# Fixed-order attention: q, k, v ahead of weights, conversions at other places, variance in PSUM, first outputs behind the last results

## The chip, the core and the metric

The kernel runs on one core of a Trainium2 chip. The metric is the device time of one execution in microseconds; the kernel before has a median of 1237.65 us over 3 runs (1236.31 to 1238.02). The engines named below are TensorE (PE, its weight loads PEld), VectorE (DVE), ScalarE (ACT), GpSimd (POOL) and SyncE (SP), whose queue issues the DMAs.

## What is computed

Three stages follow one another. All inputs and the output are float32.

```
# q, k, v: (batch 4, heads 8, seq 576, dim 64)
kv  = einsum('bhsd,bhse->bhde', k, v)
out = einsum('bhsd,bhde->bhse', q, kv)
x   = out / sqrt(mean(out*out, -1) + 1e-6) * g_norm
x   = x.transpose(0, 2, 1, 3).reshape(2304, 512)
# first feed-forward: 512 -> 2048 -> 512
h   = x @ w_in
x   = (h * clip(h + 3, 0, 6) / 6) @ w_out
# four weighted experts: 512 -> 1024 -> 512
p   = domain_probs / (domain_probs.sum(-1) + 1e-9)
y   = sum over e of p[:, e] * (relu(x @ w1[e]) @ w2[e])
```

## The kernel before, in words

The kernel works with pairs: a value is held as a high part in a rounded float32 form that PE takes at full rate, and a low part, the difference. A product of two such values is three matmuls (high-high, high-low, low-high). ACT usually writes the high part (a copy), DVE the low part (a subtraction).

**Attention.** The 4 batches times 2 halves of heads give eight steps, i = 0 to 7. att_load(i) issues three DMAs of 576 KB (q, k, v) into six rotating SBUF tiles, so the loads of step i+2 wait until step i has read its own. att_q transposes q on PE into PSUM and hands back ACT copies; att_kv forms k^T v in the PSUM tile kvp (72 small matmuls) and copies it to kvd; att_out (L233) multiplies q by kv into the PSUM tile pp, of which there is one, then ACT squares it and DVE reduces the squares. att_rms forms 1/rms in small steps (L271 to L279, 18 columns each) and scales pp into the SBUF tile xt. att_x (L283) transposes xt back on PE into PSUM tiles px (two of 512 columns, one of 128, px8), and ACT and DVE write from them the pair xH, xL that the feed-forward reads.

**Feed-forward.** w_in and w_out are cut into 16 column tiles, numbered n; each has two halves (h = 0 for w_in, h = 1 for w_out). load_raw issues the DMA of one half (512 KB, three SBUF buffers); convert(n) turns it into a pair by seven DVE operations and three ACT copies per half, written as a generator whose yields let the caller place it step by step. Where POOLED covers (n, h), the multiply and the add of that half (L161, L164) run on POOL. conv(k) takes k such yields. Tokens are cut into tiles t = 0 to 4 (512 columns, the last 256). ff_in(u, t, f) is twelve matmuls into a PSUM tile ph and a gate of four operations (L336 to L340, ACT and DVE in turn) that gives gH, gL; ff_out is twelve matmuls into four PSUM banks po, and ff_end copies them to acc for the first unit (L372) and adds them to acc for later units.

**Order.** From L462 to L539 the order of PE, ACT and DVE instructions is written out by hand (manual_schedule). Each step i of the loop from L472 takes att_out(i), the transposes of q(i+1), the small steps of 1/rms, att_kv(i+1), then filler for PE (zero matmuls, warm, in steps 0 and 1; from step 2 the first unit's ff_in, half of its matmuls in an even step and half with the gate in the odd one), then the transposes of the last result, att_x(i-1), and SLOTS[i] yields of conversion. After the eight steps att_x(7) follows; then the attention's PSUM pools close and a pool of six banks (psb) opens over their space; then ff_out(0, t) for t = 0 to 4 with the two remaining ff_in between them and conv(3) after each (L519), and small operations on domain_probs. From L541 on step(n) runs the other four units: an ff_in, an ff_out three items behind, and as much conversion as a budget allows; that part, and the experts after it, are ordered by the planner, which may move some of its instructions up into the end of the hand-written part.

Of the kernel before, what the change touches and what calls it, by code (L numbers as in the profile page):

```python
# [8 lines left out]
F32 = mybir.dt.float32  # L9
# [8 lines left out]
def kernel(  # L18
# [18 lines left out]
    nc = tc.nc  # L37
# [27 lines left out]
    PADL, PADR = 208, 248  # L65
# [25 lines left out]
    def bank_b(shape, name):  # L91
        turn[0] += 1
        return psb.tile(shape, F32, tag=f"b{turn[0] % 6}", name=name)
# [40 lines left out]
    def convert(n):  # L134
# [4 lines left out]
        for h in range(2):  # L139
# [29 lines left out]
            load_raw()  # L169
# [88 lines left out]
    def att_rms(i):  # L258
# [3 lines left out]
        va, s0, r0, ri = (sp.tile([P, NG], F32, tag=n, name=n) for n in ("va", "s0", "r0", "ri"))  # L262
# [20 lines left out]
    def att_x(i, pxs, px8):  # L283

        b, hf = divmod(i, 2)
        xt = st.pop(i)["xt"]
# [8 lines left out]
        for r in range(NP):  # L295
# [5 lines left out]
            em.append(pair(px, xH[b][:, hf * NP + r, :], xL[b][:, hf * NP + r, :]))  # L301
        nc.tensor.transpose(px8, xt[:, 2 * GA:].rearrange("p g d -> p (g d)"), ident)
# [44 lines left out]
    def ff_out(u, t, f):  # L347
# [4 lines left out]
        if f == 0:  # L352
            po_t[u, t] = [bank_b([P, TB], "po2")[:, :n] for _ in range(KD)]
# [11 lines left out]
    def ff_end(u, t):  # L365
# [42 lines left out]
    POOLED = ((0, 1), (3, 0))  # L408
# [31 lines left out]
    def warm(sizes):  # L440
        zp = psa.tile([P, DM], F32, tag="a0", name="zp")
        for n in sizes:
            nc.tensor.matmul(zp[:, :n], lhsT=zero[:, :P], rhs=zero[:, :n], start=True, stop=True)
# [404 lines left out]
```

## Time and profile before

| | |
|---|---|
| median of 3 runs | 1237.65 us |
| profiled execution | 1240.38 us, of which its span 1238.60 us |
| mean granted clock of PE | 0.937 of full speed |
| PE busy | 1209.9 us, 98% of the span |
| DVE busy | 769.6 us, 62% |
| ACT busy | 583.4 us, 47% |
| POOL busy | 14.0 us, 1% |
| moved by DMA | 87.15 MB, mean 70 GB/s |

The profile comes from one execution. Times count from the span's start. A row of the timeline gives the start, the length, the engine, the line, the operation and the tile written and read; in brackets stands how long the engine was idle before and what released it. [...]

### The profile page before, as it was taken

The page shows a single profiled execution, that of the slowest core. Times are in us where ns is not written, and L with a number is a line of the kernel's source. Part 1 is how long each engine was busy: PE and PEld are TensorE (multiplying, and loading weights), DVE is VectorE, ACT ScalarE, POOL GpSimd, SP SyncE. Part 2 cuts the span into 40 slices and gives each one's busy share as a digit, 9 for nine tenths or more (in the row PEclk, how much of TensorE's full clock was granted, in tenths as well). Part 3 has the DMA queues.
Part 4 walks back from the last instruction along what each step waited for, and adds up shares of the span by engine and source line. Part 5 has one row for each costly group of instructions (what it writes and reads, how often), then busy time and mean ns, then how long its engine had stood idle before and what let it go on. Part 6 is the DMA issues. An engine that isn't in the chain of part 4 may idle for free.

```text
span 1238.6 us, 16911 instructions
## 1 busy us (share of the span) xinstructions
PE 1209.9 (98%) x6749; PEld 1067.7 (86%) x6749; DVE 769.6 (62%) x1448; ACT 583.4 (47%) x1121; POOL 14.0 (1%) x20
## 2 busy tenths in 40 slices
PE   8978999999999999999999999999999999999997
PEld 7766888888888889999999989999999899999996
DVE  5865999783533555565656585656565856565652
ACT  5756455442322434444444554444444554444441
POOL 1100000000000000000000000000000000000000
PEclk9868999999999999999999999999999999999998
DMA  9611222210010002111212232112222321222202
GB/s 357 226 35 35 85 71 86 66 52 1 1 68 1 1 1 69 69 69 69 69 68 69 69 103 85 69 68 69 69 68 68 86 103 68 69 69 68 69 1 51
DMA packets 59343, 87.15 MB, mean 70 GB/s; under 512 B 3712, under 2 KB 36480, under 8 KB 59264
## 3 DMA queue, kind: packets, MB, share of 16 engines
q1 hardware_dynamic: 59264, 86.07, 21.0%
q8 instruction: 53, 0.87, 0.3%
q14 instruction: 26, 0.21, 0.0%
HBM read 81.34 MB, written 4.72 MB: 69 GB/s over the span
## 4 chain that ended last, share of the span: by engine, by line
PE 93%; DVE 3%; DMA 2%; ACT 1%; issue 0%; SPq 0%; POOLq 0%; POOL 0%; ACTq 0%; DVEq 0%
PE po L682 31%; PE po L358 15%; PE qa L715 14%; PE qb L715 14%; PE ph L323 5%; PE ph L324 5%; PE ph L325 5%; DMA vin<-in_v_dram 1%; DMA kin<-in_k_dram 1%; PE pp L242 1%; DVE acc L698 1%; PE kvp L224 1%; DVE xl L292 1%; PE pq L205 0%; PE px L299 0%; ACT acc L372 0%
## 5 line engine op out<-in xcount | busy, mean ns | idle before, releaser
L682 PE MATMUL po<-wout,g 128*128 128x512 f32 x1728 | 402.1, 390 | 0.0
L682 PEld LDWEIGHTS po<-wout,g 128*128 128x128 f32 x1728 | 323.6, 188 | 65.4
L715 PE MATMUL qb<-xs,win 128*128 128x384 f32 x1008 | 203.3, 336 | 1.2 <-ACT us L756 1.2
L715 PE MATMUL qa<-xs,win 128*128 128x384 f32 x1008 | 203.0, 335 | 0.0
L358 PE MATMUL po<-gH,w 128*128 128x512 f32 (+1 forms) x640 | 195.9, 372 | 4.6 <-DVE xl L292 3.0
L715 PEld LDWEIGHTS qb<-xs,win 128*128 128x128 f32 x1008 | 177.9, 188 | 3.8 <-ACT us L756 1.8
L715 PEld LDWEIGHTS qa<-xs,win 128*128 128x128 f32 x1008 | 178.2, 188 | 2.2 <-ACT us L756 0.2
L589 DVE TENSOR_TENSOR wout<-raw,wout 128x512 fp32r<-128x512 f32 x96 | 62.2, 688 | 171.0 <-ACT wout L588 171.0
L588 ACT ACTIVATE wout<-raw 128x512 fp32r<-128x512 f32 x96 | 55.4, 625 | 226.5 <-PE po L682 226.5
L358 PEld LDWEIGHTS po<-gH,w 128*128 128x128 f32 x640 | 118.3, 190 | 26.3 <-issue 3.3
L323 PE MATMUL ph<-xh,w 128*128 128x512 f32 (+1 forms) x320 | 119.6, 374 | 2.4 <-DVE r L337 2.4
L358 PE MATMUL po<-gL,w 128*128 128x512 f32 (+1 forms) x320 | 118.8, 371 | 0.0
L324 PE MATMUL ph<-xl,w 128*128 128x512 f32 (+1 forms) x320 | 118.4, 370 | 0.0
L325 PE MATMUL ph<-xh,w 128*128 128x512 f32 (+1 forms) x320 | 118.3, 370 | 0.0
L336 ACT ACTIVATE r<-ph,three 128x512 f32<-128x512 f32 (+1 forms) x80 | 51.6, 645 | 140.1 <-PE ph L325 140.0
L337 DVE SCALAR_TENSOR_TENSOR r<-r,ph 128x512 f32<-128x512 f32 (+1 forms) x80 | 50.5, 632 | 101.5 <-ACT r L336 101.2
L745 DVE SCALAR_TENSOR_TENSOR g<-sums,g 128x384 fp32r<-128x384 f32 x96 | 53.5, 558 | 81.4 <-ACT g L742 81.4
L742 ACT ACTIVATE g<-cs 128x384 fp32r<-128x384 f32 x96 | 50.4, 525 | 63.7 <-DVE cs L758 54.4
L588 ACT ACTIVATE win<-sums 128x512 fp32r<-128x512 f32 x96 | 60.7, 632 | 40.2 <-DVE sums L601 37.7
L323 PEld LDWEIGHTS ph<-xh,w 128*128 128x128 f32 x320 | 61.0, 190 | 13.6 <-DVE r L337 2.9
L745 DVE SCALAR_TENSOR_TENSOR g<-cs,g 128x384 fp32r<-128x384 f32 x96 | 53.3, 555 | 27.2 <-ACT g L742 27.2
L324 PEld LDWEIGHTS ph<-xl,w 128*128 128x128 f32 x320 | 61.0, 191 | 10.1
(106 smaller groups left out, 1260.6 us busy)
## 6 DMA issues: line engine op xcount, KB each, us to landing
raw<-in_moe_w_dram SPq DMA_DIRECT2D x96, 512.0 KB, 4.2
raw<-in_moe_w_in_dram SPq DMA_DIRECT2D x16, 512.0 KB, 3.6
raw<-in_moe_w_out_dram SPq DMA_DIRECT2D x16, 512.0 KB, 3.6
qin<-in_q_dram SPq DMA_DIRECT2D x8, 576.0 KB, 6.8
kin<-in_k_dram SPq DMA_DIRECT2D x8, 576.0 KB, 7.0
vin<-in_v_dram SPq DMA_DIRECT2D x8, 576.0 KB, 8.2
out_dram<-acc SPq DMA_DIRECT2D x36, 128.0 KB, 2.4
dp<-in_moe_domain_probs_dram SPq DMA_DIRECT2D x2, 36.0 KB, 8.5
```

Of the source, the lines that this page charges most:

```text
L323: nc.tensor.matmul(ph, lhsT=w[:, 0, c, :], rhs=xH[t][:, c, :], start=(c == 0), stop=False)
L324: nc.tensor.matmul(ph, lhsT=w[:, 0, c, :], rhs=xL[t][:, c, :], start=False, stop=False)
L325: nc.tensor.matmul(ph, lhsT=w[:, 1, c, :], rhs=xH[t][:, c, :], start=False, stop=(c == KD - 1))
L336: lambda: nc.scalar.activation(out=r, in_=ph, func=AF.Relu, bias=three[:, 0:1]),
L337: lambda: nc.vector.scalar_tensor_tensor(out=r, in0=r, scalar=6.0, in1=ph, op0=ALU.min, op1=ALU.mult),
L358: nc.tensor.matmul(po_t[u, t][o], lhsT=lhsT, rhs=rhs, start=(f == 0 and m == 0), stop=(f == UF[u] - 1 and m == 2))
L588: nc.scalar.activation(out=dst[0], in_=src, func=AF.Copy)
L589: nc.vector.tensor_tensor(out=dst[1], in0=src, in1=dst[0].bitcast(F32), op=ALU.subtract)
L682: nc.tensor.matmul(ps[i], lhsT=lhsT, rhs=w[:, f, y], start=(j == 0 and f == 0 and m == 0), stop=(j == FP - 1 and f == 1 and m == 2))
L715: nc.tensor.matmul(bank, lhsT=w[:, wy, AOP[m], c], rhs=xs[m][:, xy, c], start=first and n == 0, stop=n == 5, skip_group_check=True)
L742: nc.scalar.activation(out=g[f][:, 0, t], in_=src, func=func)
L745: nc.vector.scalar_tensor_tensor(out=g[f][:, 1, t], in0=src, scalar=0.0, in1=g[f][:, 0, t].bitcast(F32), op0=ALU.max, op1=ALU.subtract)
```

## The change

The first load of weights is issued behind q, k, v of step 0, and one load less is issued before the loop; two loads are added inside it, at steps 1 and 3. The nine yields of conversion ahead of att_q(0) go, three behind att_kv(0) become six, the yields per step change, and four instead of three follow each item of the transition. Other halves go to POOL: (0,0), (0,1), (1,0). The variance va becomes 18 columns of the PSUM tile pp. Step 1 transposes result 0 ahead of its zero matmuls, and step 7 transposes result 6 ahead of its filler and leaves that result's px8 and most of its own gate for later. Half of the first tile's outputs are formed in kvp while step 7 is being scaled, the other half in psx and psa; the last transposes go into pp. From tile 1 on DVE copies the fourth output of the first unit.

```diff
-    PADL, PADR = 208, 248
+    PADL, PADR = 232, 248
-        return psb.tile(shape, F32, tag=f"b{turn[0] % 6}", name=name)
+        return psb.tile(shape, F32, tag=f"b{(turn[0] - 1) % 6}", name=name)
...
-            load_raw()
+            if (n, h) > (0, 0):
+                load_raw()
...
-        va, s0, r0, ri = (sp.tile([P, NG], F32, tag=n, name=n) for n in ("va", "s0", "r0", "ri"))
+        s0, r0, ri = (sp.tile([P, NG], F32, tag=n, name=n) for n in ("s0", "r0", "ri"))
+        va = pp[:, 3 * TB - NG:]
...
-        for r in range(NP):
+        for r in range(len(pxs)):
...
+        if px8 is None:
+            return em
+        st.pop(i)
...
-        if f == 0:
-            po_t[u, t] = [bank_b([P, TB], "po2")[:, :n] for _ in range(KD)]
+        if f == 0 and (u, t) not in po_t:
+            po = [bank_b([P, TB], "po2")[:, :n] for _ in range(KD)]
+            po_t[u, t] = [po[o] for o in (0, 2, 3, 1)] if (u, t) == (0, 1) else po
...
-            if u == 0:
+            if u == 0 and o < KD - 1:
                 nc.scalar.activation(out=acc[t][:, o, :], in_=p, func=AF.Copy)
+            elif u == 0:
+                nc.vector.tensor_copy(out=acc[t][:, o, :], in_=p)
...
-    POOLED = ((0, 1), (3, 0))
+    POOLED = ((0, 0), (1, 1))
...
-    warm([DM] * 8)
-
-    load_raw()
+    warm((0,) * 8)
+
     att_load(0)
...
-    SLOTS = {0: 3, 1: 3, 2: 4, 3: 4, 4: 4, 5: 4, 6: 4, 7: 4}
+    SLOTS = {0: 8, 1: 2, 2: 3, 3: 0, 4: 3, 5: 1, 6: 3, 7: 0}
...
-        conv(9)
         qc = att_q(0)
...
-        warm([DM] * 6)
+        warm((0,) * 4)
         att_kv(0)
         qc[2]()
-        warm([DM] * 2)
-        conv(3)
+        warm((0,) * 2)
+        conv(6)
...
+            if i in (1, 3):
+                load_raw()
...
+            kvp = st[min(i + 1, NHB - 1)]["kvp"]
+            em = []
+            if i and not (2 <= i < NHB - 1):
+                pxs = ...
+                em = att_x(i - 1, pxs, kvp[:, 1, 2 * P:3 * P] if nxt else None)
             if i < 2:
-                warm(((480,) * 3 + (504,) * 3 + (506,) * 2, (248,) * 3 + (250,) * 3 + (288,) * 3 + (368,) * 3)[i])
+                warm(((8,) * 3 + (64,) * 3, (16,) * 3 + (32,) * 3)[i])
...
+            if 2 <= i < NHB - 1:
+                pxs = ...
+                em = att_x(i - 1, pxs, kvp[:, 1, 2 * P:3 * P])
             fin[0]()
-            fin[1]()
...
+            if nxt:
+                fin[1]()
             for m, (x, y) in enumerate(em):
                 x()
-                if m == 1:
+                if m == 1 and nxt:
                     fin[2]()
                 y()
-            fin[3]()
+            if nxt:
+                fin[3]()
             conv(SLOTS[i])
-        pxs = psk.tile([P, NP, TB], F32, tag="k", name="px")
-        for x, y in att_x(NHB - 1, [pxs[:, r] for r in range(NP)], pp[:, NG * D:NG * D + P]):
+        def first_out(o, po):
...
+            for m, (lhsT, rhs) in enumerate(((w[:, 0, sl], gH), (w[:, 0, sl], gL), (w[:, 1, sl], gH))):
+                nc.tensor.matmul(po, lhsT=lhsT, rhs=rhs, start=m == 0, stop=m == 2)
+            return lambda: nc.scalar.activation(out=acc[0][:, o, :], in_=po, func=AF.Copy)
+
+        acc[0] = accp.tile([P, KD, TB], F32, tag="acc", name="acc1")
+        for _ in range(4):
+            nc.tensor.matmul(kvp[:, 0, :P], lhsT=ident, rhs=ident, start=True, stop=True)
+        d0 = [first_out(o, kvp[:, o]) for o in range(2)]
+        for x in d0:
+            x()
+        em8 = att_x(NHB - 2, [], pp[:, NP * TB + P:NP * TB + 2 * P])
+        em = att_x(NHB - 1, [pp[:, r * TB:(r + 1) * TB] for r in range(NP)], pp[:, NP * TB:NP * TB + P])
+        d1 = [
+            first_out(2, psx.tile([P, TB], F32, tag="x", name="po1")),
+            first_out(3, psa.tile([P, TB], F32, tag="a1", name="po1"))]
+        for x, y in em8 + em:
             x()
             y()
+        for x in fin[1:]:
+            x()
+        for x in d1:
+            x()
...
-        for kind, t in (("o", 0), ("i", 3), ("o", 1), ("i", 4), ("o", 2), ("o", 3), ("o", 4)):
+        for kind, t in (("o", 1), ("i", 3), ("o", 2), ("i", 4), ("o", 3), ("o", 4)):
...
-            conv(3)
+            conv(4)
```

Each warm matmul now has 512 columns and takes its (zero) weights from another offset of the same tile.

## Rows read from the trace of the kernel before

**Rows 1.** The page's forty slices of the span, TensorE matmul, busy tenths.

```profile
PE   8978999999999999999999999999999999999997
```

**Rows 2.** Busy time by window: PE, PEld, DVE, ACT, POOL, clock, DMA share, GB/s.

```profile
19.00:27.50 8.50, 7.74 (x146) 7.05 (x145) 4.85 (x11) 4.14 (x10) 2.55 (x2) 0.95 1.04 404
27.50:35.10 7.60, 7.47 (x140) 6.52 (x139) 6.17 (x13) 6.80 (x17) 0.00 (x0) 0.95 0.99 346
35.10:43.70 8.60, 7.45 (x137) 6.49 (x137) 8.04 (x17) 6.04 (x15) 2.56 (x2) 0.95 0.83 274
43.70:52.50 8.80, 8.79 (x137) 7.63 (x137) 7.23 (x15) 6.60 (x16) 0.00 (x0) 0.77 0.61 202
52.50:61.40 8.90, 7.62 (x140) 6.56 (x139) 8.10 (x17) 6.34 (x15) 2.58 (x2) 0.95 0.52 182
61.40:71.70 10.30, 10.30 (x137) 9.06 (x137) 7.19 (x15) 6.68 (x16) 0.00 (x0) 0.65 0.01 2
71.70:80.50 8.80, 5.00 (x56) 4.30 (x55) 8.01 (x17) 4.32 (x9) 2.54 (x2) 0.90 0.19 61
...
117.30:120.50 3.20, 3.20 (x8) 2.52 (x9) 3.15 (x13) 1.68 (x4) 0.00 (x0) 0.50 0.35 122
...
130.00:170.00 40.00, 40.00 (x197) 33.85 (x196) 39.28 (x73) 20.16 (x34) 0.00 (x0) 0.95 0.26 79
```

**Rows 3.** Timeline of SP's DMA queue: start, length, engine, line, tile.

```profile
0.73 0.43 SPq L126 DMA_DIRECT2D raw<-in_moe_w_in_dram  x1
...
9.59 0.52 SPq L130 DMA_DIRECT2D raw<-in_moe_w_out_dram  x1
```

**Rows 4.** Timeline to 24 us; brackets hold idle time before, and its releaser.

```profile
4.76 0.66 ACT L145 ACTIVATE x<-raw 128x512 f32<-128x512 f32 x1 [2.53 <-DMA raw<-in_moe_w_in_dram]
...
9.22 1.28 PE L224 MATMUL kvp<-vin,kin 64*64 64x64 f32 x72 [0.21 <-DMA vin<-in_v_dram]
...
11.09 2.27 PEld L242 LDWEIGHTS pp<-kvd,qT 64*128 64x128 f32 x32 [0.36 <-ACT kvd L227]
...
23.49 1.28 PE L224 MATMUL kvp<-vin,kin 64*64 64x64 f32 x72 [0.76 <-DMA vin<-in_v_dram]
```

**Rows 5.** Timeline of attention steps 2 and 3, from 32 to 44 us.

```profile
32.81 0.18 DVE L276 SCALAR_TENSOR_TENSOR va<-va,r 128x18 f32<-128x18 f32 x1
...
40.29 1.29 POOL L164 TENSOR_TENSOR r<-r,a 128x512 f32<-128x512 f32 x1
...
40.80 0.82 DVE L276 SCALAR_TENSOR_TENSOR va<-va,r 128x18 f32<-128x18 f32 x1
...
43.71 1.87 PEld L242 LDWEIGHTS pp<-kvd,qT 64*128 64x128 f32 x32 [1.40 <-DVE xt L266]
```

**Rows 6.** Timeline of the transition, from 79 to 118 us.

```profile
79.04 1.42 DVE L266 TENSOR_TENSOR xt<-pp,ri 128x512 f32<-128x512 f32 x2
...
82.69 1.57 PEld L299 LDWEIGHTS px<-ident,xt 128*128 128x128 f32 x8 [6.24 <-DVE xl L292]
...
87.83 0.76 PE L358 MATMUL po<-gH,w 128*128 128x512 f32 x1 [2.95 <-DVE xl L292]
...
102.08 0.63 ACT L166 ACTIVATE w<-r 128x512 fp32r<-128x512 f32 x1 [3.89 <-POOL r L164]
...
117.30 0.29 PEld L323 LDWEIGHTS ph<-xh,w 128*128 128x128 f32 x1 [2.87 <-DVE r L337]
```

**Rows 7.** Groups by line to 88 us: busy, mean ns of one, idle before.

```profile
L292 DVE SCALAR_TENSOR_TENSOR xl<-px,gcol,xh 128x512 fp32r<-128x512 f32 x16 | 11.4, 746 | 7.3 <-ACT xh L291 7.2
...
L155 DVE SCALAR_TENSOR_TENSOR a<-raw,x 128x512 uint32<-128x512 uint32 x5 | 3.5, 691 | 0.1
...
L158 DVE TENSOR_SCALAR x<-a 128x512 uint32<-128x512 uint32 x5 | 2.1, 427 | 0.2
```

**Rows 8.** The chain of waits: start, length, engine, tile, line, count.

```profile
135.45 2.72 PE po L358 x12
```

More of the change, by code (lines that the diff above doesn't have):

```diff
@@ L285, in att_x @@
         b, hf = divmod(i, 2)
-        xt = st.pop(i)["xt"]
+        xt = st[i]["xt"]
         em = []
@@ L439, with warm @@
     nc.vector.memset(zero.bitcast(F32), 0.0)
[L440 to L443, printed above, removed]
-    warm([DM] * 8)
-    load_raw()
+    def warm(starts):
+        z = psa.tile([P, DM], F32, tag="a0", name="zp")
+        for o in starts:
+            nc.tensor.matmul(z, lhsT=zero[:, o:o + P], rhs=zero, start=True, stop=True)
+    warm((0,) * 8)
     att_load(0)
@@ L492 @@
             fin = [nop] * 4
+            kvp = st[min(i + 1, NHB - 1)]["kvp"]
+            em = []
+            if i and not (2 <= i < NHB - 1):
+                pxs = [pool.tile([P, TB], F32, tag=tag, name="px") for pool, tag in ((psx, "x"), (psa, "a1"))]
+                em = att_x(i - 1, pxs, kvp[:, 1, 2 * P:3 * P] if nxt else None)
             if i < 2:
-                warm(((480,) * 3 + (504,) * 3 + (506,) * 2, (248,) * 3 + (250,) * 3 + (288,) * 3 + (368,) * 3)[i])
+                warm(((8,) * 3 + (64,) * 3, (16,) * 3 + (32,) * 3)[i])
             elif i % 2 == 0:
@@ L498 @@
                 fin = ff_in(0, i // 2 - 1, 0, later=True, cs=(2, 3))
+            if 2 <= i < NHB - 1:
+                pxs = [pool.tile([P, TB], F32, tag=tag, name="px") for pool, tag in ((psx, "x"), (psa, "a1"))]
+                em = att_x(i - 1, pxs, kvp[:, 1, 2 * P:3 * P])
             fin[0]()
-            fin[1]()
-            em = []
-            if i:
-                pxs = [pool.tile([P, TB], F32, tag=tag, name="px") for pool, tag in ((psx, "x"), (psa, "a1"))]
-                em = att_x(i - 1, pxs, st[min(i + 1, NHB - 1)]["kvp"][:, 0, 2 * P:3 * P])
+            if nxt:
+                fin[1]()
             for m, (x, y) in enumerate(em):
                 x()
-                if m == 1:
+                if m == 1 and nxt:
                     fin[2]()
                 y()
-            fin[3]()
+            if nxt:
+                fin[3]()
             conv(SLOTS[i])
-        pxs = psk.tile([P, NP, TB], F32, tag="k", name="px")
-        for x, y in att_x(NHB - 1, [pxs[:, r] for r in range(NP)], pp[:, NG * D:NG * D + P]):
-            x()
-            y()
+        def first_out(o, po):
+            gH, gL = gt[0, 0, 0]
+            w = W[0, 0][:, 1]
+            sl = slice(o * P, (o + 1) * P)
+            for m, (lhsT, rhs) in enumerate(((w[:, 0, sl], gH), (w[:, 0, sl], gL), (w[:, 1, sl], gH))):
[13 more added lines that the diff above has]
+        for x, y in em8 + em:
+            x()
+            y()
+        for x in fin[1:]:
+            x()
+        for x in d1:
+            x()
+        gt.pop((0, 0, 0))
         done[0] = True
```

## The prediction, on record before the result was known

> **What bounds the kernel now.** I read the page's slices first: from the fifth slice on, at 124 us, PE is full but for the last [rows 1]. The stretches by window confirm it: from 130 to 170 us PE is busy for all 40.00 us at a granted clock of 0.95, though DVE is at 39.28 beside it [rows 2]. Nothing in the diff alters PE's work there, so the change can only move the point at which that full stretch begins. Before it lie the eight attention steps and the transition into the expert loop, and there I read the timeline.
>
> An attention step is one closed loop over the single PSUM tile pp: PE writes att_out, ACT squares, DVE reduces, forms 1/rms and scales, and only then may PE write the next att_out. Where nothing disturbs it a step takes 7.6 us, with PE busy 7.47 of it (27.5 to 35.1) [rows 2]: loop and PE are nearly equal. The other windows are cut at the same point of the following steps: 8.6, 8.8, 8.9, 10.3, and 8.8 for step 7 to the end of its scaling. (Step 1, 19.0 to 27.5, is 8.5.) [...] In steps 3 and 5 (35.1 and 52.5) PE idles, and its next weight load waits 1.40 us for DVE's scaling [rows 5]. [...]
>
> **The start.** The first raw weights land ahead of q, k, v: ACT takes them at 4.76, and kv of step 0 waits for v until 9.22; step 1 waits for v of step 2 until 23.49 [rows 4]. Four raw loads of 512 KB stand before the third set of q, k, v in SP's queue, the first and the fourth in [rows 3]; after the change two do. What one costs: from the first v at 9.22 to the third at 23.49 six q/k/v tiles of 576 KB and three raw ones landed, 4992 KB in 14.27 us, so 512 KB take 1.5 us. First kv 1.5 us earlier, less a little for the first landing: I take 1.4, bounds 0.8 and 1.5. The third v comes 2 x 1.5 = 3.0 earlier, at 20.5. att_out(0) would stand at about 9.7, att_out(1) some 8 later, and kv(2) some 3.6 behind that (att_out and the q transposes), at 21.3: no wait for v. Step 1 at 7.6 instead of 8.5 returns 0.85, a little under the difference. With conv(9) gone from ahead of q, ACT is free when kv ends; att_out(0) began 1.87 after kv began [rows 4], and I keep that. Behind these, load_raw at steps 1 and 3 stands after a q, k, v set in SP's queue; what it waits for (a free third buffer, then half (0,1)'s conversion in step 1) is done by then, and the next set behind it is not needed for a step or more. Cost 0; if that cover went, 1.5 per raw load.
>
> **Conversions.** One half costs DVE four operations of 0.69 and three of 0.43 [rows 7], 4.05 us; a half whose multiply and add go to POOL, 2.67. Counting yields, before the transition 42 slots become 26: DVE work in attention goes from 4.05 + 4 x 2.67 = 14.7 to 3 x 2.67 + 0.43 = 8.4 us, and step by step what is left (at most 1.1 us of slots beside the last result's xl on even steps, a GLU and no DVE slot beside it on odd ones) fits into the roughly 3 us between one scaling and the next reduction. That removes the late reductions of steps 3, 5 and 7. [...] Attention: steps 3 and 5, 1.0 + 1.3; steps 4 and 6, 1.2 + 2.7; step 7, 8.8 to 7.4, 1.4; with the start 1.4 + 0.85 this is 9.8. Against it step 0: PE's warming matmuls fall from eight to six there and the first conversions now sit in front of the first reduction, 0 to 0.4 later. I take 9.7; bounds 5 (odd steps stay as long, and the dips behind them) and 12 (PE's own 7.3 or so per step, were its small waits to go).
>
> **Variance in PSUM.** L276 has two SBUF inputs. Alone it takes 0.18; beside POOL's L164, which runs to 41.58, it takes 0.82 and ends at 41.62 [rows 5]. That is 0.64 in the loop, three times in the attention. With va in PSUM only one input is SBUF; the gain is inside the step times above. Cost of PSUM operands: the same form takes 0.691 from SBUF (L155) and 0.746 with a PSUM input (L292) [rows 7], so 0 to 0.055 for each of four operations per step: 0 to 1.8 us over eight steps; I take 0, since the 0.13 between 7.6 and PE's 7.47 covers most of it. [...] The pads grow by 96 bytes as va's tile leaves, which only moves addresses: 0.
>
> **The tail.** Now: scaling of step 7 begins its first half at 79.04 and ends 1.42 later, at 80.46; its transposes start at 82.69 after 6.24 idle, at the lower clock, waiting for DVE's xl; the first tile's outputs wait until 87.83 for the last xl (PSUM banks) [rows 6]; ACT waits 3.89 for POOL at 102.08 while finished outputs queue behind it; the loop's third ff_in stands at 117.30 for L337 [rows 6], and the next 3.2 us run at 0.50 [rows 2], losing 3.2 x (1 - 0.50/0.95) = 1.5. From 80.46 to full PE: 36.8 + 1.5 = 38.3 us.
>
> After: four identity products and half of tile 0's outputs fill PE while step 7 scales; the transposes go straight into pp as the scaling ends. PE then has nine transposes (about 1.1; 1.57 at the lower level), six output matmuls (1.36), three full output sets and ff_in(0,3) at 2.72 each [rows 8], two half-width sets at 1.4 and two hoisted ff_in of the loop: 1.1 + 1.36 + 10.88 + 2.8 + 5.44 = 21.6 us. DVE has in that stretch four xl (3.0), two small ones (0.7), three GLU pairs, one of half width (3.6), the moved o=3 copies (2.5) and 24 slots of conversion, none on POOL (3.6 + 4.1 + 3.4 = 11.1 for what is left of half (1,1), for (2,0) and for most of (2,1)): 20.9, and six waits of 0.63 [rows 6] for the high part that ACT writes between two dependent DVE operations, three in GLUs and three in conversions, 3.8: 24.7. So DVE, not PE, ends this stretch; L337 comes 0.7 later, 25.4, and the stall of 3.8 may again cost 1.5 of clock: 26.9. Gain 38.3 - 26.9 = 11.4. Bounds: 16.7 if PE is never held, 4 if ACT's queue of copies, conversions and GLU leaves only the POOL wait saved. The deferred GLU of tile 2 is wanted two items later; the copies moved to DVE shorten ACT by three of twelve full ones.
>
> **Sum.** 9.7 + 11.4 = 21.1. The profiled execution took 1240.38 (span 1238.60 and 1.78 around it), so 1219.3; it lies 2.73 above the median of the runs shown, and I predict 1237.65 - 21.1 = 1216.5.
>
> **Rivals.**
> (a) The conversions sent back hold the transition: DVE and ACT alternate as now and the tail gives only 4: 1237.65 - 13.7 = 1224. For: DVE's count already exceeds PE's there. Against: the POOL wait and the bank wait do go.
> (b) Odd attention steps stay DVE-bound at 8.6 to 8.9 (GLU plus xl leave no room in the 3 us), and the clock still dips behind them: 5 + 11.4 = 16.4, 1221.
> (c) DVE becomes the pace-maker of the stretch to 170: it is 39.28 of 40 busy there and receives 6.3 us more (14.7 - 8.4) and 2.8 of multiplies and adds that POOL did, while PE arrives 21 us earlier. If the end of that stretch is DVE's, all is given back: 1237.5. Against: conversions are rationed per step, PE shows no wait there, and the weights of the third unit are due only ten steps into the loop.
> [...]
>
> **How the numbers follow.** Chances: forecast 0.61 (its own range 1210 to 1221.5), (a) 0.16, (b) 0.09, (c) 0.04, (d) 0.05, and 0.05 for better than 1210, with the transition fully hidden. The range 1209 to 1226 takes in (a) and (b) and leaves out (c), (d) and the far ends. About 0.2% (2.5 us) is what a measurement of this kernel can tell from no change: faster 0.91, same 0.04, slower 0.05.
>
> **What would show it.** Right: kv of step 0 near 7.8 and no DMA wait at kv(2); att_out starts 7.5 to 7.7 apart from step 2 on, clock 0.95 throughout; L276 at about 0.2 whatever POOL does; step 7's scaling ending near 70.7; PE full from about 97. Wrong: att_out distances of 8.6; clock rows under 0.9 between 10 and 70; a long wait of PE for DVE or ACT between 72 and 97; or PE idle behind 100, which is (c).

## The result, and the profile after

The changed kernel took 1218.83 us, the median of four runs (1218.57 to 1219.55); the kernel before took 1237.84 (1236.31 to 1241.34) on the same chip. The ratio is 0.9843 [0.9822, 0.9865]: 19.0 us less, where 21.1 were forecast. The two profiled executions differ by 21.9 us in span (1238.6 and 1216.7), close to the sum that was made against the first of them. The kernel before is the less steady of the two: beside the experiments below, its 23 executions with a mean granted clock (a share of full speed, as the profile gives it) of 0.987 or 0.988 took 1240.2 to 1244.2 us and its ten with 0.990 or 0.991 took 1237.2 to 1239.7, so what the lower clock costs it is not the same each time; the 21.9 are counted against an execution of 1240.38 us. (Repeated later, the same kernel had 1218.52 and a ratio of 0.9829 [0.981, 0.9848].)

Where the time came from is read from landmarks in each trace: the starts of att_out, the end of step 7's scaling, and the loop's third ff_in; all in us.

| | before | after | gain |
|---|---|---|---|
| start to att_out(0) | 11.09 | 9.52 | 1.57 |
| att_out(0) to att_out(1) | 7.98 | 7.89 | 0.09 |
| to att_out(2) | 8.42 | 8.16 | 0.26 |
| to att_out(3) | 7.59 | 7.37 | 0.22 |
| to att_out(4) | 8.63 | 7.36 | 1.27 |
| to att_out(5) | 8.81 | 7.37 | 1.44 |
| to att_out(6) | 8.85 | 7.38 | 1.47 |
| to att_out(7) | 10.34 | 7.36 | 2.98 |
| to the end of step 7's scaling | 8.75 | 7.32 | 1.43 |
| attention, in all | 80.46 | 69.73 | 10.73 |
| from there to the loop's third ff_in | 36.84 | 26.81 | 10.03 |
| from there to the end of the span | 1121.3 | 1120.2 | 1.1 |

The page's slices of the kernel after, matmul busy tenths and granted clock: the 7 and the 8 of the third and fourth slice [rows 1] are gone, no slice of the clock lies under 9, and PE is full from the second slice on.

```profile
PE   8999999999999999999999999999999999999997
PEclk9999999999999999999999999999999999999999
```

Busy time by window of the kernel after: PE, PEld, DVE, ACT, POOL, clock, DMA share, GB/s. The first three are attention steps 2, 3 and 6, the next four the transition (whole, then in three parts), the last two the expert loop.

```profile
25.60:33.00 7.40, 7.40 (x140) 6.48 (x139) 5.22 (x12) 4.29 (x11) 0.00 (x0) 1.00 1.01 380
33.00:40.40 7.40, 7.40 (x139) 6.48 (x139) 6.50 (x15) 6.68 (x16) 0.00 (x0) 1.00 1.01 327
...
55.10:62.40 7.30, 7.30 (x138) 6.40 (x137) 6.59 (x14) 6.23 (x15) 0.00 (x0) 1.00 0.01 2
...
69.73:96.54 26.81, 22.82 (x112) 18.14 (x113) 19.02 (x36) 17.01 (x35) 0.00 (x0) 1.00 0.13 41
...
69.70:75.90 6.20, 3.36 (x19) 2.69 (x20) 3.70 (x8) 3.04 (x6) 0.00 (x0) 1.00 0.00 0
75.90:90.00 14.10, 14.10 (x68) 11.55 (x69) 10.34 (x19) 8.38 (x16) 0.00 (x0) 1.00 0.18 57
90.00:96.50 6.50, 5.37 (x27) 3.90 (x26) 4.97 (x11) 5.58 (x12) 0.00 (x0) 1.00 0.12 43
...
102.00:142.00 40.00, 40.00 (x190) 33.57 (x188) 39.08 (x75) 21.18 (x35) 0.00 (x0) 1.00 0.26 79
130.00:170.00 40.00, 40.00 (x195) 33.82 (x194) 38.39 (x73) 20.68 (x34) 0.00 (x0) 1.00 0.23 71
```

Step 3, which had 1.15 us of idle PE, and step 6, which had a clock of 0.65 [rows 2], are now free of both: PE is busy for the whole step. The loop is not far behind it, since the first weight load of steps 3 and 4 still waits 0.21 us for the scaling. The transition has 26.81 - 22.82 = 3.99 us of idle PE left, in its first and its last part. In the loop DVE is at 39.08 of 40, and PE is still busy for all of it.

The timeline of the first steps of the kernel after: start, length, engine, line, operation, tile.

```profile
7.65 1.28 PE L225 MATMUL kvp<-vin,kin 64*64 64x64 f32 x72
...
14.38 1.28 PE L225 MATMUL kvp<-vin,kin 64*64 64x64 f32 x72 [0.88 <-DMA vin<-in_v_dram]
14.41 1.27 POOL L164 TENSOR_TENSOR r<-r,a 128x512 f32<-128x512 f32 x1
...
15.10 0.18 DVE L278 SCALAR_TENSOR_TENSOR pp<-pp,r 128x18 f32<-128x18 f32 x1
...
21.25 1.28 PE L225 MATMUL kvp<-vin,kin 64*64 64x64 f32 x72 [0.22 <-DMA vin<-in_v_dram]
```

kv of step 0 starts at 7.65 instead of 9.22 and that of step 2 at 21.25 instead of 23.49 [rows 4], with 0.22 of waiting for v left. L278, which was L276, takes 0.18 while POOL's L164 runs from 14.41 to 15.68; beside the same operation it took 0.82 [rows 5].

The end of the transition in the kernel after, ACT, DVE and PE:

```profile
71.20 0.37 ACT L293 ACTIVATE xh<-pp,gcol 128x128 fp32r<-128x128 f32 x1 [0.57 <-PE pp L307]
...
71.99 0.69 ACT L293 ACTIVATE xh<-pp,gcol 128x512 fp32r<-128x512 f32 x1 [0.42 <-DVE xl L294]
...
75.90 0.47 PE L364 MATMUL po<-gH,w 128*128 128x512 f32 x1 [2.66 <-DVE xl L294]
...
91.46 1.55 ACT L378 ACTIVATE acc<-po 128x512 f32<-128x512 f32 x3
...
92.89 0.68 ACT L145 ACTIVATE x<-raw 128x512 f32<-128x512 f32 x1
...
94.01 0.95 ACT L378 ACTIVATE acc<-po 128x256 f32<-128x256 f32 x3
...
94.81 0.73 ACT L341 ACTIVATE r<-ph,three 128x512 f32<-128x512 f32 x1
...
95.81 0.68 DVE L342 SCALAR_TENSOR_TENSOR r<-r,ph 128x512 f32<-128x512 f32 x1
...
96.54 0.19 PEld L328 LDWEIGHTS ph<-xh,w 128*128 128x128 f32 x1 [1.60 <-DVE r L342]
96.54 0.50 PE L328 MATMUL ph<-xh,w 128*128 128x512 f32 x1 [1.18 <-DVE r L342]
```

PE waits 2.66 us for the last low parts of the results at 75.90, and 1.18 at the third ff_in (96.54) for the gate's L342; its weight load there waits 1.60, where it waited 2.87 before [rows 6]. The rest of the 3.99, 0.15 us, lies ahead of the first transposes, at 69.88. Weight loads also wait for ACT in three places (0.41 us at 86.66 and at 91.61, 0.19 at 92.09), but the busy time of PE's matmuls shows no gap there.

### The profile page after: what moved, and what is told of

It reads as the page before. It is cut to its first block, busy times and chain, and to the rows that moved or that the text cites. A ratio compares the mean times of both kernels' runs of the same rounds, so it can differ in the third digit from the quotient of the medians.

```text
span 1216.7 us, 16908 instructions
## 1 busy us (share of the span) xinstructions
PE 1200.5 (99%) x6747; PEld 1059.8 (87%) x6747; DVE 770.7 (63%) x1456; ACT 582.7 (48%) x1117; POOL 8.9 (1%) x16
## 4 chain that ended last, share of the span: by engine, by line
PE 95%; DVE 2%; DMA 1%; ACT 1%; issue 0%; SPq 0%; DVEq 0%; ACTq 0%
PE po L721 32%; PE po L364 15%; PE qa L754 14%; PE qb L754 14%; PE ph L328 5%; PE ph L330 5%; PE ph L329 5%; PE pp L243 1%; DMA vin<-in_v_dram 1%; DVE acc L737 1%; DMA qin<-in_q_dram 1%; PE kvp L225 1%; PE px L301 0%; PE pq L206 0%; PE pp L250 0%
## 5 line engine op out<-in xcount | busy, mean ns | idle before, releaser
L364 PE MATMUL po<-gH,w 128*128 128x512 f32 (+1 forms) x632 | 192.1, 368 | 2.7 <-DVE xl L294 2.7
L364 PEld LDWEIGHTS po<-gH,w 128*128 128x128 f32 x632 | 115.7, 188 | 23.4 <-issue 3.1
L364 PE MATMUL po<-gL,w 128*128 128x512 f32 (+1 forms) x316 | 116.3, 368 | 0.0
L342 DVE SCALAR_TENSOR_TENSOR r<-r,ph 128x512 f32<-128x512 f32 (+1 forms) x80 | 50.5, 631 | 87.1 <-ACT r L341 86.8
L328 PEld LDWEIGHTS ph<-xh,w 128*128 128x128 f32 x320 | 60.3, 189 | 12.3 <-DVE r L342 1.6
L330 PEld LDWEIGHTS ph<-xh,w 128*128 128x128 f32 x320 | 60.3, 188 | 10.1
```

The lines of the kernel that those rows point to most:

```text
L328: nc.tensor.matmul(ph, lhsT=w[:, 0, c, :], rhs=xH[t][:, c, :], start=(c == 0), stop=False)
L330: nc.tensor.matmul(ph, lhsT=w[:, 1, c, :], rhs=xH[t][:, c, :], start=False, stop=(c == KD - 1))
L342: lambda: nc.vector.scalar_tensor_tensor(out=r, in0=r, scalar=6.0, in1=ph, op0=ALU.min, op1=ALU.mult),
L364: nc.tensor.matmul(po_t[u, t][o], lhsT=lhsT, rhs=rhs, start=(f == 0 and m == 0), stop=(f == UF[u] - 1 and m == 2))
```

## Experiments

Each kernel was timed beside the kernel before on the same chip, and a ratio has that before under it. The intervals are 0.2 to 0.4% wide on either side, so between two experiments only differences above some 3 us are told by ratios; smaller ones are read from the traces, at the end of step 7's scaling ("scaling", 69.73 in the kernel after) and at the span (1216.7). Traces differ by chance too: att_out(0) starts anywhere from 9.52 to 10.17 in the ten profiled executions with the new load order, and from 10.83 to 11.09 in the four with the old. The kernel after is at the early end, so a landmark "later" by some 0.2 to 0.6 us can be this alone.

**The weights loaded first again.** From the kernel after:

```diff
+    load_raw()
     att_load(0)
...
-            if (n, h) > (0, 0):
-                load_raw()
+            load_raw()
...
-            if i in (1, 3):
-                load_raw()
```

> The changed kernel with its load order undone alone: the first raw weights ahead of q, k, v again, three raw loads before the loop, none added in steps 1 and 3. Theory (the load order is a term of its own): kv of step 0 waits for v until about 9.2 instead of 7.65, kv(2) waits for v until 23 or so, steps 3 to 7 keep their 7.4 us, so that the scaling of step 7 ends 1.5 to 3 us later than at 69.7 and the median is 1220.3 to 1222. Rival (the closed loop of the steps sets the pace and swallows the later landing): scaling of step 7 ends within 0.5 us of 69.7, median 1218.8.

It took 1221.79 us, ratio 0.9849 [0.9824, 0.9874]; scaling ended at 71.21. kv of step 0 moved from 7.65 to 9.05, as the row shows:

```profile
9.05 1.28 PE L224 MATMUL kvp<-vin,kin 64*64 64x64 f32 x72 [0.64 <-DMA vin<-in_v_dram]
```

So the first load's place is worth 1.4 us at the first kv, as forecast, and 1.5 at the end of the attention: the second and third v cost nothing further, since here too the first two steps are 7.9 and 8.2 long. The span was 2.6 longer (1219.3); what is beyond these 1.5 lies in the transition, where PE waited 2.64 us for xl and behind it, from 77.94 to 79.65, started a matmul of 512 columns every 0.43 us, where it started one every 0.23 from 80.45 on.

**The old yields per step.** And POOL again for all halves from (0,0) to (2,1). From the kernel after:

```diff
-    POOLED = ((0, 0), (1, 1))
+    POOLED = ((0, 0), (3, 0))
...
-    SLOTS = {0: 8, 1: 2, 2: 3, 3: 0, 4: 3, 5: 1, 6: 3, 7: 0}
+    SLOTS = {0: 3, 1: 3, 2: 4, 3: 4, 4: 4, 5: 4, 6: 4, 7: 4}
```

> The changed kernel with the conversion slots per step of the kernel before (3, 3, then 4 in each step) and POOL again for all halves up to (2,1); everything else as changed. Theory (conversions make the odd steps late, the idle makes the clock fall in the steps behind them, and POOL holds the transition): steps 3, 5 and 7 take 8.2 to 8.8 us instead of 7.4, the granted clock falls under 0.9 in at least one step behind, the scaling of step 7 ends 4 to 8 us later, and ACT waits about 4 us for POOL in the transition; median 1225 to 1230. Rival (the conversions cost only their own lateness, the clock stays): each of three steps 0.5 us longer, 1220 to 1221.

It took 1240.07 us, ratio 0.9989 [0.9974, 1.0003]: the whole gain was gone, far beyond what was expected. Steps 3 to 7 took 10.3 to 10.7 us. The timeline of step 3 and the window of step 4 say why:

```profile
37.61 1.27 POOL L164 TENSOR_TENSOR r<-r,a 128x512 f32<-128x512 f32 x1
38.91 0.63 ACT L166 ACTIVATE w<-r 128x512 fp32r<-128x512 f32 x1 [3.99 <-POOL r L164]
39.45 1.18 ACT L255 ACTIVATE xt<-pp 128x512 f32<-128x512 f32 x2
...
44.50:54.80 10.30, 10.30 (x137) 8.98 (x137) 7.99 (x17) 6.75 (x16) 0.00 (x0) 0.67 0.41 130
```

With the nine yields ahead of the loop gone and these counts in it, the pair of POOL operations and the copy that needs them now fall into one step: ACT waits 3.99 us for POOL, and the squares of the result (L255), on the attention's closed loop, stand behind that copy in ACT's queue. PE idles, and the step behind each such step runs at a clock of 0.67. This run tells nothing of the number of yields. Beside the next one, which differs from it by five yields in step 0 alone, it shows that their phase against the steps decides.

**The old number of yields, in the old phase.** The same edit, but step 0 keeps its eight:

```diff
-    POOLED = ((0, 0), (1, 1))
+    POOLED = ((0, 0), (3, 0))
...
-    SLOTS = {0: 8, 1: 2, 2: 3, 3: 0, 4: 3, 5: 1, 6: 3, 7: 0}
+    SLOTS = {0: 8, 1: 3, 2: 4, 3: 4, 4: 4, 5: 4, 6: 4, 7: 4}
```

> The changed kernel with four conversion slots per step and POOL for all halves up to (2,1), as before the change, but with the slots in the phase that they had there: POOL's multiply and add stand at the end of an even step and ACT's high copy of the same half a step later (in e2 both fell in one step). Theory (what cost e2 most was ACT's queue, whose squares stood behind a copy that waits for POOL; with the phase right only DVE's lateness is left): no step of 10 us, steps 3, 5 and 7 at 7.9 to 8.4, scaling of step 7 ends 2 to 6 us later than at 69.7, ACT waits for POOL once in the transition; 0.9880 to 0.9920 of the kernel before. Rival (four slots as such are too many for the step): scaling of step 7 ends over 10 us later, 0.995 or more.

It took 1221.93 us, ratio 0.9867 [0.9829, 0.9905]; scaling ended at 72.76, 3.0 later, and the tail gave 0.9 back (span 1218.8). Step 4, by window:

```profile
41.27:49.33 8.06, 7.49 (x138) 6.48 (x138) 7.29 (x16) 7.61 (x18) 0.00 (x0) 1.00 0.83 271
```

Steps 3, 4 and 6 take 8.05 us with 0.57 of PE idle ahead of the next, and in this execution no clock drops in the attention (one of the four executions, not profiled, took 1226.35 us at a mean clock of 0.993). So fewer conversions, with fewer halves on POOL, are worth 3 us there with the rest of the change in place, 2.8 counted from att_out(0).

**The conversions alone, in the kernel before.**

```diff
-    POOLED = ((0, 1), (3, 0))
+    POOLED = ((0, 0), (1, 1))
...
-    SLOTS = {0: 3, 1: 3, 2: 4, 3: 4, 4: 4, 5: 4, 6: 4, 7: 4}
+    SLOTS = {0: 8, 1: 2, 2: 3, 3: 0, 4: 3, 5: 1, 6: 3, 7: 0}
...
-        conv(9)
         qc = att_q(0)
...
-        conv(3)
+        conv(6)
...
-            conv(3)
+            conv(4 if (kind, t) != ("o", 0) else 0)
```

> The kernel before with only the conversions placed as after the change (none ahead of q, six behind the first kv, 8, 2, 3, 0, 3, 1, 3, 0 per step, POOL for (0,0), (0,1), (1,0), 24 slots in the transition); loads, va and the transition's first part as before. Theory (conversions in the attention and POOL in the transition are the largest single part): steps 3 and 5 at 7.6 to 7.9 and no lower clock in steps 4 and 6, though POOL's add may now hold DVE in steps 0, 1 and 5; no wait of ACT for POOL in the transition; 8 to 12 us faster, 0.9900 to 0.9935. Rival (the parts need each other): under 4 us.

It took 1232.35 us, ratio 0.9934 [0.991, 0.9958]; scaling ended at 73.76, 6.7 earlier than before. Steps 5 and 6, by window:

```profile
49.29:57.49 8.20, 7.39 (x137) 6.44 (x137) 7.59 (x15) 6.30 (x15) 2.56 (x2) 1.00 0.52 194
57.49:66.39 8.90, 8.89 (x137) 7.80 (x138) 6.61 (x14) 5.60 (x14) 0.00 (x0) 0.81 0.01 2
```

Steps 2 to 4 are at 7.42, but step 5, the one in which POOL works, still has 0.81 of PE idle, and step 6 behind it a clock of 0.81; this lower clock was not expected. The span (1228.9) is 9.7 shorter, so 3.0 lie behind the scaling, where POOL no longer works and ACT's wait of 3.89 for it [rows 6] is gone. How much of these 3.0 is the edit's stays open: the kernel with only the variance moved (below) has the transition of the kernel before and is 2.2 shorter there.

**The variance in SBUF again.** From the kernel after:

```diff
-    PADL, PADR = 232, 248
+    PADL, PADR = 208, 248
...
-        s0, r0, ri = (sp.tile([P, NG], F32, tag=n, name=n) for n in ("s0", "r0", "ri"))
-        va = pp[:, 3 * TB - NG:]
+        va, s0, r0, ri = (sp.tile([P, NG], F32, tag=n, name=n) for n in ("va", "s0", "r0", "ri"))
```

> The changed kernel with va in SBUF again. Theory (an operation of DVE with two SBUF inputs stands behind POOL's add, a PSUM operand costs nothing that counts): the operation that multiplies va by r0 takes 0.4 to 0.8 us instead of 0.18 in steps 0, 1 and 4, where POOL's add runs at that time; steps 0 and 4 hand on about 0.5 us each, step 1 has slack; median 1219.4 to 1220. Rival (the PSUM operands cost 0.055 us each in four operations of eight steps): 1.8 us faster, 1217.

It took 1222.28 us, ratio 0.9854 [0.983, 0.9878]; scaling ended at 72.74, 3.0 later: the right direction, and more than expected. Two steps with POOL at work, and the group of the operation that was hit:

```profile
22.25 1.28 POOL L164 TENSOR_TENSOR r<-r,a 128x512 f32<-128x512 f32 x1
22.81 0.74 DVE L274 TENSOR_SCALAR va<-ssq 128x18 f32<-128x18 f32 x1
...
54.16 1.29 POOL L164 TENSOR_TENSOR r<-r,a 128x512 f32<-128x512 f32 x1
54.22 1.26 DVE L274 TENSOR_SCALAR va<-ssq 128x18 f32<-128x18 f32 x1
...
L274 DVE TENSOR_SCALAR va<-ssq 128x18 f32<-128x18 f32 x8 | 3.1, 382 | 0.3
```

In these two steps it is not the operation of [rows 5], with two SBUF inputs, that waits (it is L277 here, and took 0.64 in step 0), but the one two ahead of it, L274, with one input: it starts while POOL's L164 runs and ends when that ends (23.55 and 55.48 against 23.53 and 55.45). It takes 0.18 alone, 0.74 and 1.26 beside POOL; by what means the one holds up the other was not shown. In the kernel after, where its output va lies in PSUM, the same operation (L275) starts at 21.99, between the start of L164 at 21.70 and its end at 22.97, and takes 0.18.

**The variance in PSUM alone, in the kernel before.** The reverse of that edit.

```diff
-    PADL, PADR = 208, 248
+    PADL, PADR = 232, 248
...
-        va, s0, r0, ri = (sp.tile([P, NG], F32, tag=n, name=n) for n in ("va", "s0", "r0", "ri"))
+        s0, r0, ri = (sp.tile([P, NG], F32, tag=n, name=n) for n in ("s0", "r0", "ri"))
+        va = pp[:, 3 * TB - NG:]
```

> The kernel before with only va moved to PSUM. Theory (POOL's add holds an operation with two SBUF inputs in steps 3, 5 and 7, and the idle time of PE that this leaves is part of what makes the clock fall): L276 takes 0.18 in every step, steps 3, 5 and 7 are 0.6 shorter, PE's wait ahead of steps 4 and 6 falls from 1.4 to 0.8; if that no longer lowers the clock, steps 4 and 6 return to 7.6 and all is 5 us or more faster (0.996 or less); if it still does, 1.9 us (0.9985). Rival (PSUM operands cost as much as the hold): no change.

It took 1234.32 us, ratio 0.9957 [0.9937, 0.9977]; scaling ended at 74.53, 5.9 earlier than before. Step 4, which followed an idle stretch and ran at 0.77 [rows 2], by window:

```profile
43.10:51.10 8.00, 7.41 (x139) 6.50 (x139) 7.34 (x16) 7.56 (x18) 0.00 (x0) 1.00 0.79 268
```

PE's weight loads now wait at most 0.94 us for the scaling, where one waited 1.40 [rows 5], and the clock stays up through all of the attention. Moving 18 columns, with the conversions untouched, removes both dips in this execution. It is the fastest of eight (1232.27 to 1237.56 us, mean clocks from 0.994 down to 0.988), and whether the slower ones dip in the attention was not seen; the ratio puts the gain over all of them at 5.3 us, with an interval of 2.9 to 7.8. In the traces this edit gives 5.9 us of the attention alone and the conversions 6.7; with the other in place each gives 3.0. Counted from att_out(0) it is 5.7 and 6.5 alone, 2.6 and 2.8 with the other. They are largely substitutes for each other.

**No zero matmuls in steps 0 and 1.** From the kernel after:

```diff
             if i < 2:
-                warm(((8,) * 3 + (64,) * 3, (16,) * 3 + (32,) * 3)[i])
+                pass
```

> The changed kernel without the zero matmuls in steps 0 and 1 (twelve; no result of them is used). Theory (an idle PE lowers the clock in the stretch behind): PE idles over 2 us in steps 0 and 1, the granted clock is under 0.9 in step 1 or 2, that step is 1 to 3 us longer, and the scaling of step 7 ends as much later. Rival (the steps' own matmuls hold the clock, or DVE's loop hides it): clock 1.00 throughout, end within 0.5 us.

It took 1220.84 us, ratio 0.9845 [0.9812, 0.9878]; scaling ended at 72.49, 2.8 later. Step 1 and what follows it, by window:

```profile
17.40:25.50 8.10, 7.53 (x86) 6.90 (x90) 5.25 (x13) 4.30 (x9) 2.53 (x2) 0.50 1.05 405
25.50:33.00 7.50, 7.50 (x179) 6.82 (x171) 5.43 (x10) 4.96 (x12) 0.00 (x0) 0.86 0.81 292
33.00:40.40 7.40, 7.40 (x149) 6.47 (x141) 6.38 (x15) 6.24 (x15) 0.00 (x0) 1.00 0.93 296
```

Rival (d), chance 0.05, is a clock that falls early and stays low. The fall is real: PE waited 1.71 us for the scaling ahead of step 1, and step 1 then took 10.36 us, at a clock of 0.50 for all of the first window. But with step 2, in which ff_in fills PE, the clock comes back and stays through the attention. Nor does every execution fall: two of the four took 1222.6 us at a mean clock of 0.992, the profiled one among them (some 1.7 of its excess is a spell behind the last xl, as in the control below), and the other two 1218.1 and 1219.1 at 0.998 and 0.997, no slower than the kernel after.

**The tail as before.** From the kernel after, the last transposes in kvp's place and the first outputs behind them:

```diff
-                em = att_x(i - 1, pxs, kvp[:, 1, 2 * P:3 * P] if nxt else None)
+                em = att_x(i - 1, pxs, kvp[:, 1, 2 * P:3 * P])
...
-        d0 = [first_out(o, kvp[:, o]) for o in range(2)]
...
+        pxs = psk.tile([P, NP, TB], F32, tag="k", name="px")
+        for x, y in att_x(NHB - 1, [pxs[:, r] for r in range(NP)], pp[:, NG * D:NG * D + P]):
...
-        for kind, t in (("o", 1), ("i", 3), ("o", 2), ("i", 4), ("o", 3), ("o", 4)):
+        for kind, t in (("o", 0), ("i", 3), ("o", 1), ("o", 2), ("i", 4), ("o", 3), ("o", 4)):
...
-            conv(4)
+            conv(4 if (kind, t) != ("o", 0) else 0)
```

> The changed kernel with the transition's first part undone: the last transposes go into the tile of kvp again, all of the first tile's outputs are formed after the last results in the six-bank pool, the gate of tile 2 is not deferred; conversions, loads and va as changed. Theory (PE's empty stretch behind the last scaling is the larger part of the transition's gain): PE waits some 5 us around 70 to 77, runs at the lower clock behind, first outputs start 7 us after the scaling ends, and full PE begins 5 to 9 us later; median 1224 to 1228. Rival (DVE's conversions end the transition whatever PE does before): at most 2 us later, 1219 to 1221.

It took 1225.52 us, ratio 0.9879 [0.9856, 0.9903]; the span was 6.6 longer, of which 0.5 arose before the end of the scaling (70.22). The first wait and the two windows behind it:

```profile
72.44 1.97 PE L301 MATMUL px<-ident,xt 128*128 128x128 f32 x8 [4.64 <-DVE xl L294]
...
70.20:77.00 6.80, 2.18 (x9) 1.78 (x9) 3.87 (x8) 2.52 (x5) 0.00 (x0) 0.51 0.00 0
77.00:82.00 5.00, 4.43 (x14) 3.61 (x15) 0.72 (x3) 1.79 (x3) 0.00 (x0) 0.65 0.01 3
```

The old wait for xl is back, and the lower clock with it. So undoing this part of the transition's edits costs 6.1 us; DVE's copy of the fourth output, the four yields per item and POOL's places stay as changed here, and the last items stand in a slightly other order than before the change.

**What is left in the tail.** Four kernels on one chip. The first is the changed kernel once more, as a control.

> The changed kernel once more, unaltered, on the same chip as the three that follow, as their yardstick: 0.984 of the kernel before, scaling of step 7 ends near 69.7, third ff_in of the loop starts near 96.5, PE waits 2.7 us at 73 to 76 for the last xl.

It took 1218.52 us. In its profiled execution the wait for xl was 2.65 us long, as in the first profile, but here the clock fell behind it:

```profile
76.40:79.00 2.60, 2.54 (x8) 2.06 (x9) 1.20 (x2) 2.06 (x5) 0.00 (x0) 0.67 0.00 0
79.00:82.00 3.00, 3.00 (x11) 2.39 (x10) 1.94 (x4) 1.00 (x3) 0.00 (x0) 0.72 0.00 0
```

By these two clocks that cost 2.6 x 0.33 + 3.0 x 0.28 = 1.7 us, and the execution took 1220.32, 1.8 above the median of its runs; the other three took 1218.2 to 1218.5.

The second splits the PSUM tile pp in two, so that the first half's ACT copy need not wait for an operation on the other half:

```diff
-    pp = psp.tile([P, 3 * TB], F32, name="pp")
+    ppa = psp.tile([P, TB], F32, name="ppa")
+    ppb = psp.tile([P, 2 * TB], F32, name="ppb")
...
-        em8 = att_x(NHB - 2, [], pp[:, NP * TB + P:NP * TB + 2 * P])
-        em = att_x(NHB - 1, [pp[:, r * TB:(r + 1) * TB] for r in range(NP)], pp[:, NP * TB:NP * TB + P])
+        em8 = att_x(NHB - 2, [], ppb[:, TB + P:TB + 2 * P])
+        em = att_x(NHB - 1, [ppa, ppb[:, :TB]], ppb[:, TB:TB + P])
```

> The changed kernel with pp as two PSUM tiles (one bank, two banks) instead of one of three banks. Theory (waits on PSUM go by whole tiles: ACT's and DVE's turns on the last three results follow one another because all lie in pp, and the second set of outputs waits for the last of them though its bank is free): the high copy of the first 512 columns no longer waits for the small xl, PE's wait of 2.7 us at 73 to 76 falls to 1.5 or less, and all that follows comes 0.5 to 1.5 us earlier; 1.0 us faster than e9. Rival (the turns are set by the engines' order, the wait by DVE): no change within 0.3 us.

It took 1216.13 us (1215.65 to 1216.61), ratio 0.9807 [0.9788, 0.9825], 2.4 below the control. The high copy and PE's wait:

```profile
71.58 0.68 ACT L298 ACTIVATE xh<-ppa,gcol 128x512 fp32r<-128x512 f32 x1
...
74.63 0.47 PE L369 MATMUL po<-gH,w 128*128 128x512 f32 x1 [0.53 <-DVE xl L299]
```

The 2.65 become 0.53. In the unsplit kernel the same copy waited 0.42 for the small low part at 71.99, and each of the four results in pp then waited for the one before, ACT and DVE in turn; this is what the 2.66 at 75.90 were made of. From the scaling to the third ff_in the split kernel needs 24.79 us against 26.81 in the kernel after, 2.0 less.

The third gives all of the first unit's copies to ACT again:

```diff
-            if u == 0 and o < KD - 1:
+            if u == 0:
                 nc.scalar.activation(out=acc[t][:, o, :], in_=p, func=AF.Copy)
-            elif u == 0:
-                nc.vector.tensor_copy(out=acc[t][:, o, :], in_=p)
```

> The changed kernel with the fourth output of the first unit's tiles copied by ACT again instead of DVE. Theory as on record (DVE ends the transition): ACT's queue has room, the third ff_in starts no later or up to 1 us earlier, 0 to 1 us faster than e9. Rival (ACT's queue of copies, conversions and gates ends it, since the third ff_in waits for a gate whose first half ACT took 3 us after its product was complete): third ff_in 1 to 2.5 us later, as much slower.

It took 1222.85 us, ratio 0.986 [0.9841, 0.9878], 4.3 above the control. The third ff_in, and the clock behind it:

```profile
98.54 0.50 PE L328 MATMUL ph<-xh,w 128*128 128x512 f32 x1 [2.25 <-DVE r L342]
...
98.50:101.00 2.50, 2.46 (x8) 2.01 (x9) 2.50 (x7) 1.45 (x3) 0.00 (x0) 0.72 0.48 163
101.00:103.00 2.00, 2.00 (x7) 1.54 (x6) 1.96 (x11) 0.68 (x1) 0.00 (x0) 0.50 0.00 0
```

From scaling to the third ff_in this kernel needs 28.11 us against 26.81, 1.3 more, and the wait of 2.25 is followed by a spell of lower clock that by its two windows costs 2.5 x 0.28 + 2.0 x 0.50 = 1.7. Together 3.0. The profiled execution was itself 1.2 below this kernel's median; where the other executions lost that was not seen. DVE had less to do here and ACT more, and the stretch became longer: ACT's queue holds it at least as much as DVE's.

The fourth is the second with one more copy per tile on DVE, from tile 3 on:

```diff
-            po_t[u, t] = [po[o] for o in (0, 2, 3, 1)] if (u, t) == (0, 1) else po
+            po_t[u, t] = [po[o] for o in (0, 2, 1, 3)] if (u, t) == (0, 1) else po
...
-            if u == 0 and o < KD - 1:
+            if u == 0 and o < (KD - 1 if t < 3 else KD - 2):
```

> e10 and two more steps: of the last two tiles of the first unit DVE copies two outputs instead of one, and the third output of tile 1 takes the bank that is free early. If ACT's queue ends the transition: third ff_in 0.5 to 1.5 us earlier than in e10, 1.5 to 2.5 us faster than e9. If DVE ends it: later than e10 by up to 1 us.

It took 1215.79 us (1215.43 to 1216.54), ratio 0.9805 [0.9787, 0.9823]; 0.3 below the second, which the ranges of the two do not separate. The gate ahead of the third ff_in:

```profile
92.29 0.75 DVE L385 COPY acc<-po 128x256 f32<-128x256 f32 x2
...
93.28 0.68 DVE L347 SCALAR_TENSOR_TENSOR r<-r,ph 128x512 f32<-128x512 f32 x1
...
94.02 0.50 PE L333 MATMUL ph<-xh,w 128*128 128x512 f32 x1 [1.29 <-DVE r L347]
```

ACT's part of this gate was done at 92.14, and DVE reached its own, behind the copies, at 93.28; in the kernel after ACT's was done at 95.54 and DVE's began at 95.81. So work taken from ACT only moved the last wait to DVE: there the two are about in balance. The two kernels that split pp are faster than the changed one and the one before.

## Why the prediction came out right, point by point

**Start.** Right: 1.4 forecast at kv of step 0, 1.57 found in all, and 1.4 to 1.5 when the one edit was undone. These pairs flatter it a little: over all profiled executions the new order has att_out(0) at 9.81 on average and the old at 10.94, 1.1 apart. Step 1 was to return 0.85 and returned 0.26: kv of step 2 started 2.2 earlier, where v was to come 3.0 earlier, and still waited 0.22 for it, and 8.16 us is no loop-bound step, since PE there also has the first result's transposes (0.41 of idle that the profile puts down to nothing) and the zero matmuls.

**Conversions and dips.** Right in mechanism: steps 3 to 7 gained 1.27, 1.44, 1.47, 2.98 and 1.43, where 1.0, 1.2, 1.3, 2.7 and 1.4 were forecast. The idle went, and the lower clock with it: 0.77 and 0.65 in steps 4 and 6 before, each behind a step in which PE idled [rows 2], 1.00 in both after. The steps became 7.3 to 7.4 rather than 7.5 to 7.7, because little is left in them but PE's own work. What the prediction did not see is that the conversions are not the only cure and, without the other, not a full one. It gave them nearly all the credit; the runs show that the variance in PSUM alone, which it named for 0.64 in three steps without a term of its own, gives 5.9 us and took away both dips in its profiled execution, that the conversions alone give 6.7 and leave a clock of 0.81 in step 6, and that undoing either now costs only 3.0. Rival (b) is thereby refuted, and the phase of the yields, which no rival named, turned out to be the mechanism that could have taken all the gain back (ratio 0.9989).

**Variance in PSUM.** The cost was taken at 0 with a bound of 1.8. The groups of the kernel after, over the attention: busy, mean ns, idle before.

```profile
L278 DVE SCALAR_TENSOR_TENSOR pp<-pp,r 128x18 f32<-128x18 f32 x8 | 1.5, 185 | 0.3
L280 DVE TENSOR_TENSOR pp<-pp,s 128x18 f32<-128x18 f32 x8 | 1.5, 184 | 0.3
...
L342 DVE SCALAR_TENSOR_TENSOR r<-r,ph 128x512 f32<-128x512 f32 x2 | 1.4, 676 | 0.0
```

L280 had taken 178 ns with va in SBUF and takes 184 with it in PSUM, and the reciprocal behind it, which reads va and writes to SBUF, 266 and 271; the four operations together lose about 20 ns a step, 0.2 us in eight. No price of PSUM was found for the operation of 512 columns, L342, which reads PSUM and takes 676 against 691 for the same kind from SBUF [rows 7]; the kernel before had the same operation at 677 (L337). So the 55 ns by which xl is longer, and which the prediction took for the price of PSUM, were not shown to be that price; their cause stays open.

**Tail.** The term came out by luck. To the third ff_in 25.4 were forecast and 26.81 found, 1.4 too little; behind it 1.5 of lower clock were forecast and none came, so the two errors cancel in the forecast 26.9. Up to there PE's work is 22.8 (21.6 forecast) and its idle 3.99 (3.8). But the step that said "DVE, not PE, ends this stretch" failed: DVE is busy for 19.02 of the 26.81 us, not 20.9 and full. The idle is not one stall at the end but a wait of 2.66 for the results in the undivided pp, which the split cut to 0.53, and 1.18 at the end, where ACT's queue and DVE's come out level. The 1.5 us of lower clock were put behind a stall at that end. Nothing fell there, but behind the wait of 2.65 in the control 1.7 were lost, so it was no wrong price but one that is not always paid. Rival (a), 4 us for the tail, is refuted by 10.0.

**Sum.** 21.1 were forecast and 21.9 found between the two profiled executions, and the prediction's 1219.3 for such an execution is near the measured 1218.83. The 1216.5 that it put down is 2.3 too low: it took the gain off the median of the kernel before, though part of the gain is lower clock, of which the faster executions of that kernel, by their mean clocks, pay less.

**DVE in the loop.** Rival (c) is refuted: DVE is at 39.08 of 40 us and PE at 40.00.

**Clock.** Rival (d) did not come about: in the profiled execution of the kernel after the clock never fell in the attention, 1.00 in every step. That a fallen clock stays low through the attention is refuted too: without the zero matmuls the clock did fall in the profiled execution, and one step cost 2.2 us more, but it recovered in the next.

## What to carry to other kernels

Where two engines alternate on one tile, look first for small operations that a third engine delays: with 18 columns no longer held for 0.64 us by POOL, and nothing else changed, the step after ran at full clock and 0.8 us shorter in the execution that was profiled. Work that is interleaved by counting steps has a phase as well as an amount; when the amount is changed, check in which step each of its waits falls. And where a wait is set by a whole tile, the tile can be split: that gave 2.4 us here, while of the copies moved between engines one in four was worth 4.3 and a second one nothing that could be told.

## What the runs showed of the hardware

A granted clock of 0.95 and one of 1.00 went with the same work: 12 matmuls take 2.72 us in both kernels [rows 8], and 40 us hold 197 and 195 of them [rows 2]. So those two readings are not 5% apart in time. At 0.50 the work did take longer: in the kernel before, matmuls of 512 columns started 0.43 us apart at that clock (from 118.32 to 120.03), and 0.23 apart once it was back (from 120.74 to 121.66). A mean between these readings can be a mixture: step 4 of the kernel before, 0.77 as a whole [rows 2], reads 0.95 in the microsecond from 44, then 0.71, 0.50, 0.50 and 0.55, and 0.95 again from 49 on. Nor do 0.95 and 1.00 belong to a kernel: two executions of the kernel before, of 1240.38 and 1240.22 us, have mean clocks of 0.937 and 0.987. From the chain of the kernel after:

```profile
107.73 2.72 PE po L364 x12
```

Seven profiled executions have the changed transition with the undivided pp, and in it a wait of PE of 2.6 to 2.9 us for the last xl. In three of them (the control, the weights first, no zero matmuls) a spell near half clock followed, with matmuls of 512 columns 0.43 us apart, in four none. After 4.6 us, 2.25 us and, ahead of step 1 without zero matmuls, 1.71 us there was one, and after 1.18 us none. Shorter waits are no surer: ahead of step 6, one of 0.81 us with the conversions alone was followed by a clock of 0.81, and one of 0.85 with the variance in SBUF again by 1.00. Here the length of a single idle spell did not by itself tell whether the clock would fall.

The matmuls of the rounded high and low parts were the quicker ones by the column. At a clock of 1.00 in the kernel after, one of 256 columns came every 0.12 us (from 90.07 to 90.31), and a transpose of 128 columns of unrounded float32 every 0.11 (eight from 31.82 to 32.69).
